# Retention and a three-way maxout layer on one core: a weight load cut in two, and two blocks' small loads moved up the SP queue

## Chip, core and metric

The kernel runs on one core of a Trainium2 chip. The metric is the time of one execution on the device, in microseconds (us); the time of a kernel is the median of its runs. Profiles are of one execution each, with the hardware profiler.

## What is computed

Eight batches of eight heads of linear attention with decay (retention) over 576 positions and 64 channels, then a feed-forward layer whose hidden unit is the largest of three projections. The weights arrive as 64-bit floats, everything else as 32-bit floats.

```python
batch, n_heads, seq, head_dim = (8, 8, 576, 64)
n_tokens, d_model, d_ff = (4608, 512, 768)
...
scores = scale * np.matmul(q, k.transpose(0, 1, 3, 2))
Dmat = np.where(rel >= 0, gamma[:, None, None] ** rel[None, :, :], 0.0)
ret = scores * Dmat[None, :, :, :]
attn = np.matmul(ret, v)
...
h = np.maximum(np.maximum(x @ w1, x @ w2), x @ w3)
return h @ w_out
```

`x` is the attention's output with the heads side by side: 4608 rows of 512.

## The kernel before

**Blocks and tiles.** The 4608 rows are cut into 36 blocks of 128 rows, and four blocks make one tile of 512 rows. `ffn(t)` is the feed-forward layer of tile t. While it runs, `steps(t + 1)` works on the attention of the next tile's four blocks, in twelve places: place n is a list of steps, emitted ahead of the n-th part of `ffn(t)`. All engines run what is emitted for them strictly in that order. Tile 0's blocks 0 to 3 are done before any feed-forward work. Blocks 4 to 7 (called a, b, c, d in `steps(1)`) are done during `ffn(0)`, and this is also the time in which the weights are loaded and converted.

**Loads.** All loads of q, k, v and of the weights are issued by SP, one after the other.

- `load` (L247) brings k, q and v of blocks 0 to 3, and k and v of later blocks, 256 KB each, in rows of 256 bytes.
- `load_blocks` (L229) brings q and k of blocks from 4 on once more, in 32x32 pieces as VectorE's transpose wants them: sixteen transfers of 32 KB a block (eight of q, eight of k), in rows of 128 bytes. Their two buffers each are used in turn, so block 7's wait for block 5's transposes and block 6's for block 4's.
- `load_weights(n)` (L520, L516) goes on by n pieces in a list. Two pieces are a pair: of w1, w2 or w3, a pair is 256 columns, 1 MB, loaded by one transfer in rows of 2 KB when its first piece comes up; the second piece then loads nothing. Of w_out, a pair is two transfers of 512 KB. There are nine pairs of w1, w2, w3 and three of w_out, and four buffers for pairs. Each conversion of a pair asks for the next two pieces (`product`).
- A transfer carries one of eight semaphores in turn, and its issue waits until the transfer eight before it has landed.

**Conversion.** `convert_all` makes 32-bit floats of a pair of 64-bit ones, in small steps spread over `ffn(0)`: on ACT two activations that read the loaded words (L695, L696) and two more (L702, L704); on VectorE L703, L708, L713 and L728. The first three pairs are converted by halves (one piece at a time), all others whole. The first pair's first half is needed by the first product of the feed-forward layer (`up_plain`, L858).

**Attention of blocks 0 to 3.** TensorE transposes k and q (`kt`, `qt`, L286), ACT copies them to SBUF (L287), TensorE makes scores (L300), VectorE masks them (L216), and TensorE makes the new state (`kv`, L368) and the output (`o`, L409, and L424 for the part that comes from the state).

**Attention of blocks from 4 on.** `transposes` is two transposes on VectorE (`kT`, `qT`, L216). `decay` scales v: of blocks 4 and 5 in one operation on VectorE (L254), of later blocks in eight operations on ACT (L204, one a head), which wait in a list that `scale` empties a few at a time, in between the conversion's activations; `scores` first empties what is left. Then, for each head in turn, TensorE makes the scores (`sk`, L322) and the state's increment (`kv`, L325), which needs that head's scaled v. Blocks 6 and 7 come one after the other, just ahead of the last product of the layer, `downs_plain` (`down`, L845), which goes through w_out's pairs in order with sixteen matmul instructions a pair; the attention's outputs of blocks 6 and 7 (`o`, L439 and L446) stand after the first pair.

**Order on SP.** At the start: k, q, v of blocks 0 and 1; k and q of block 2; the first weight pair; v of block 2; k, q, v of block 3; the next two pairs. Later, from the last pair of w3 on: w_out's first pair; k and v of block 6; w_out's second pair; k and v of block 7; the sixteen small loads of block 6; w_out's third pair; the sixteen of block 7; then block 8's.

Of the kernel before, what the change touches and what calls it, by code (L numbers as in the profile page):

```python
# [98 lines left out]
def kernel(  # L99
# [14 lines left out]
    nc = tc.nc  # L114
    P = 128
# [7 lines left out]
    CPT = NT // C  # L123
# [62 lines left out]
    def spans(g):  # L186

        row = 0
        while row < C:
            b, pos = divmod(g * C + row, S)  # L190
            n = min(C - row, S - pos)
            yield row, b, pos, n
            row += n
# [24 lines left out]
    def load_blocks(g, *blocks):  # L218
        for n, src in (("q", q), ("kx", k)):

            if 0 in blocks:
                raws[n, g] = raw.tile([P, H, D // 32, 32], FP32, tag=n, name=n + "raw", bufs=2)
            t = raws[n, g]
            for blk in blocks:
                b, pos = divmod(g * C + 32 * blk, S)
                c, e = divmod(blk, 2)
                for a in range(2):
                    r = D * c + 32 * a
                    nc.sync.dma_start(  # L229
                        t[r:r + 32, :, e, :],  # L230
                        src[b, :, pos:pos + 32, 32 * a:32 * a + 32].rearrange("h p i -> p h i"))

    def load(g, names="kqv"):
        if g >= BY_PE and "q" in names and ("q", g) not in raws:
            load_blocks(g, *range(C // 32))
        for n, src in (("k", k), ("q", q), ("v", v)) if g < BY_PE else (("k", k), ("v", v)):
            if n not in names:
                continue
            bufs = {"k": 3, "q": 2, "v": 4}[n]
            pool, bufs = (raw0, 1) if n != "v" and g < BY_PE and g % (bufs + 1) == bufs else (raw, bufs)  # L240
            if n == "v":
                t = vpool.tile([C, H, D], FP32, tag="v", name="vraw")
            else:
                t = pool.tile([C, H, D], FP32, tag=n, name=n + "raw", bufs=bufs)
            raws[n, g] = t
            for row, b, pos, m in spans(g):
                nc.sync.dma_start(t[row:row + m], src[b, :, pos:pos + m, :].rearrange("h p d -> p h d"))  # L247
# [252 lines left out]
    WS = (moe_w1, moe_w2, moe_w3)  # L500
    units = [(fp, i) for fp in range(NF // 2) for i in range(3)]
# [5 lines left out]
    def load_weights(n):  # L507
        for _ in range(n):
            if not to_load:
                return  # L510
            i, fb = piece = to_load.popleft()
            if fb % 2 == 0:
                bits[i, fb // 2] = wraw.tile([P, 2, DM], I64, tag="bits", name="bits")
            t = bits[i, fb // 2]
            if i == "out":
                nc.sync.dma_start(t[:, fb % 2, :], moe_w_out[fb * P:(fb + 1) * P, :])  # L516
                continue
            if fb % 2:
                continue
            nc.sync.dma_start(t[:].rearrange("p e f -> p (e f)").rearrange("p (n f) -> p n f", f=2 * P),  # L520
                              WS[i][:, fb * P:(fb + 2) * P].rearrange("(n p) f -> p n f", p=P))

    def seven_forms(order):

# [148 lines left out]
    def convert_all():  # L673
# [3 lines left out]
        class Two:  # L677
# [38 lines left out]
            def product(self, e):  # L716
                mant, expo = self.of(e, self.mant, self.expo.bitcast(FP32))
                if self.i == "out":
                    w = w_out[:, self.fp]
                    both_of = w.rearrange("p e f -> p (e f)")  # L720
                else:
                    w = w_up[self.i][:, 2 * self.fp:2 * self.fp + 2, :]
                    both_of = w.rearrange("p e (n f) -> p n e f", f=P)
                    if e is both:
                        mant, expo = (x.rearrange("p (n e f) -> p n e f", e=2, f=P) for x in (mant, expo))
                    else:
                        both_of = both_of[:, :, e, :]
                nc.vector.tensor_tensor(both_of, mant, expo, op=ALU.mult)  # L728
                for n in (0, 1) if e is both else (e,):
                    w_sb[self.i, 2 * self.fp + n] = w[:, n, :]  # L730
                    load_weights(1)
# [121 lines left out]
    def up_plain(t, h, fb, i, *parts):  # L853
        ps = (ps_x, ps_y)[fb % 2].tile([P, NT], FP32, tag="xy"[fb % 2], name="up")

        def products(a, b):
            for dc in range(NDC):
                nc.tensor.matmul(ps[:, a:b], lhsT=w_sb[i, fb][:, dc * P:(dc + 1) * P], rhs=xT[t][:, dc, a:b],  # L858
                                 start=dc == 0 and a == 0, stop=dc == NDC - 1, skip_group_check=len(parts) > 0)

        def maximum():
            if i > 0:
                nc.vector.tensor_tensor(h[:, fb, :], h[:, fb, :], ps[:], op=ALU.max)
            else:
                nc.scalar.copy(h[:, fb, :], ps[:])

        ends = [0, *parts, NT]
        steps = [partial(products, a, b) for a, b in zip(ends, ends[1:])]
        steps.pop(0)()
        return (*steps, maximum)  # L870
# [113 lines left out]
    load(0)  # L984
    load(1)
    load(2, "kq")
    load_weights(2)
    load(2, "v")
    load(CPT - 1, "kqv")
    load_weights(2)  # L990
    load_weights(2)
    decay(0)
# [35 lines left out]
    def steps(t):  # L1028


        todo = [[] for _ in range(3 * CPT)]

        def at(n, *what):
            for step, *args in what:
                if step is values:
                    if args[0][0] < NG:
                        todo[n].append(partial(values, *args))
                elif args[0] < NG:
                    todo[n].append(partial(soon, partial(step, *args)) if step is load else partial(step, *args))

        if t == 1:
            a, b, c, d = range(CPT, 2 * CPT)
            at(0, (load, a, "kv"))
            at(1, (load_blocks, a, 0, 1, 2, 3))
            at(2, (load_weights, 2))
            at(3, (load, b, "kv"), (load_blocks, b, 0, 1, 2, 3), (decay, a))
            at(4, (transposes, a))
            at(5, (load, c, "kv"), (decay, b), (transposes, b))
            at(6, (load, d, "kv"), (decay, c), (load_blocks, c, 0, 1, 2, 3))
            at(7, (values, [a, b]), (decay, d), (convert, 2), (load_blocks, d, 0, 1, 2, 3))  # L1050
            at(8, (transposes, c))
            at(9, (load, d + 1))
            at(10, (values, [c, d]), (load_blocks, d + 2, 0, 1))
            at(11, (decay, d + 1), (load_blocks, d + 2, 2, 3), (load, d + 2), (transposes, d + 1))
            return todo
        for n in range(0, CPT, 2):
            a, b, m = CPT * t + n, CPT * t + n + 1, 6 * (n // 2)
            first_pair = t == 2 and n == 0
            s = m + 2 if first_pair else m + 1
            at(m - (n > 0), (transposes, b))  # L1060
            if first_pair:
                at(m, (decay, b), (load, a + 2))
            at(s, (scores, a), (scores, b), (load, b + 2))
            at(s + 1, (decay, a + 2))
            at(s + 2, (decay, b + 2))
            at(s + 3, (values, [a, b]), (transposes, a + 2), (load, a + 4))
        return todo

    for t in range(N // NT):
        work = ffn(t)  # L1070
        for todo in steps(t + 1):
            for step in todo:
                step()
            next(work, None)
# [51 lines left out]
```

## Time and profile before

| | |
|---|---|
| median of 3 runs | 740.69 us (738.68 to 741.06) |
| the profiled execution's own time | 739.48 us |
| its span | 737.8 us |
| granted TensorE clock | 1.0 of full speed |
| attention of blocks 0 to 3 and the first pair's conversion | 0 to 27 us |
| `ffn(0)`, with blocks 4 to 7 and the conversion of all weights | 22 to 118 us |
| tiles 1 to 8 | 118 us to the end |

How to read it: the span is what the profile covers, from the first to the last instruction, and the execution's time is a little longer. PE is TensorE's matmuls, PEld its weight loads, DVE is VectorE, SPq the issuing of transfers on SP. A row of the timeline has start and duration in us, the engine, line and operation, what it writes and reads, the sizes, and how often it ran in a row; in brackets stands how long the engine had been idle before it, and who released it. A row of the waits has who waited for whom, the us in total, how often, and the longest. An issue on SP takes as long as SP is held up by it, waits included.

The page's share of the transfers and of VectorE and ACT in 40 slices of the span (18.4 us each, in tenths):

```profile
DVE  4899799999886895689658876787768966893676
ACT  4795905554345524544354535543555255424441
DMA  9878544414251415141424243322514151000001
```

The first six slices, up to 118 us, hold the most transfers, and VectorE and ACT are at their fullest there.

### The profile page before, as it was taken

What the parts mean: (1) busy time and instruction counts of PE and PEld (TensorE: products, weight loads), DVE (VectorE), ACT (ScalarE), POOL (GpSimd) and SP (SyncE); (2) the same over time, 40 slices, a digit from 0 to 9 for tenths busy, and PEclk for the clock granted to TensorE, in tenths of its full rate; (3) what the DMA queues carried; (4) which work ended last, traced back from release to release, by engine and by line L of the source; (5) the groups of instructions that cost most, each with busy time, mean ns of one, the idle gap of its engine ahead of it and who ended that gap; (6) DMA issues with size and microseconds to landing.
All of it is one profiled execution on the core that took longest, in us unless ns stands there. A gap on an engine that the chain in (4) does not pass through costs nothing.

```text
span 737.8 us, 17257 instructions
## 1 busy us (share of the span) xinstructions
PE 731.2 (99%) x6916; PEld 604.5 (82%) x6916; DVE 575.3 (78%) x1050; ACT 352.2 (48%) x734; POOL 37.1 (5%) x43
## 2 busy tenths in 40 slices
PE   9999999999999999999999999999999999999998
PEld 7644546888888888888888888888888888888887
DVE  4899799999886895689658876787768966893676
ACT  4795905554345524544354535543555255424441
POOL 2000010112000100010000000000100010000000
DMA  9878544414251415141424243322514151000001
GB/s 234 270 225 248 113 85 119 83 27 92 70 103 23 95 40 105 36 84 48 102 51 77 47 109 60 65 52 59 114 26 91 44 106 26 1 29 30 1 1 57
DMA packets 234832, 59.90 MB, mean 81 GB/s; under 512 B 220672, under 2 KB 228864, under 8 KB 234752
## 3 DMA queue, kind: packets, MB, share of 16 engines
q1 hardware_dynamic: 233776, 58.76, 35.3%
q8 instruction: 54, 0.88, 0.5%
q14 instruction: 26, 0.21, 0.1%
q10 hardware_dynamic: 976, 0.04, 0.1%
HBM read 49.32 MB, written 9.44 MB: 80 GB/s over the span
## 4 chain that ended last, share of the span: by engine, by line
PE 91%; SPq 5%; DMA 2%; DVE 1%; issue 0%; DVEq 0%
PE a L833 20%; PE b L833 17%; PE c L833 9%; PE di L666 7%; PE d L833 6%; PE e L833 6%; PE dhc L666 5%; PE up L858 3%; PE deg L666 3%; SPq L229 3%; PE sk L322 3%; PE down L845 3%; PE o L439 2%; PE o L446 2%; PE dfd L666 2%; PE dx L573 1%
## 5 line engine op out<-in xcount | busy, mean ns | idle before, releaser
L821 DVE TENSOR_TENSOR part<-part 128x512 f32<-128x512 f32 x168 | 117.8, 701 | 85.9 <-ACT part L818 83.3
L818 ACT COPY part<-b 128x512 f32<-128x512 f32 x120 | 70.3, 586 | 163.2 <-PE b L833 162.7
L821 DVE TENSOR_TENSOR h<-h,part 128x512 f32<-128x512 f32 x120 | 83.2, 694 | 23.8 <-ACT h L818 19.8
L204 ACT ACTIVATE vraw<-vraw,gk 128x64 f32<-128x64 f32 x240 | 77.0, 347 | 11.3 <-DMA vraw<-in_v_dram 11.3
L818 ACT COPY part<-a 128x512 f32<-128x512 f32 x96 | 56.3, 586 | 51.5 <-PE a L833 51.1
L833 PE MATMUL b<-s,n 128*128 128x256 f32 x288 | 73.9, 379 | 0.0
L858 PE MATMUL up<-xT,w 128*128 128x512 f32 (+2 forms) x160 | 62.9, 552 | 0.0
L833 PEld LDWEIGHTS b<-s,n 128*128 128x128 f32 x288 | 54.7, 190 | 7.4
L858 PEld LDWEIGHTS up<-xT,w 128*128 128x128 f32 x160 | 28.8, 190 | 31.5 <-issue 28.6
L339 POOL TENSOR_TENSOR s<-s,gs_of 64x512 f32<-64x512 f32 x24 | 26.4, 1101 | 552.3 <-DVE s L337 512.1
L833 PE MATMUL c<-xT,w 128*128 128x256 f32 x192 | 51.3, 389 | 0.0
L655 ACT COPY k<-di 128x256 f32<-128x256 f32 x49 | 18.3, 373 | 68.5 <-PE di L666 42.1
L833 PE MATMUL d<-s,w 128*128 128x256 f32 x192 | 49.8, 380 | 0.0
L833 PE MATMUL b<-xT,n 128*128 128x256 f32 x192 | 49.3, 379 | 0.0
L833 PE MATMUL a<-xT,w 128*128 128x256 f32 x192 | 49.3, 379 | 0.0
L833 PE MATMUL a<-s,w 128*128 128x256 f32 x192 | 49.3, 379 | 0.0
L833 PE MATMUL a<-xT,n 128*128 128x256 f32 x192 | 45.4, 379 | 0.0
L833 PE MATMUL e<-xT,w 128*128 128x256 f32 x192 | 45.4, 379 | 0.0
L833 PEld LDWEIGHTS e<-xT,w 128*128 128x128 f32 x192 | 36.5, 190 | 5.4 <-issue 0.5
L833 PEld LDWEIGHTS b<-xT,n 128*128 128x128 f32 x192 | 36.5, 190 | 5.0
L833 PEld LDWEIGHTS a<-xT,n 128*128 128x128 f32 x192 | 36.5, 190 | 5.0
L833 PEld LDWEIGHTS a<-xT,w 128*128 128x128 f32 x192 | 36.5, 190 | 5.0
(183 smaller groups left out, 1378.6 us busy)
## 6 DMA issues: line engine op xcount, KB each, us to landing
bits<-in_moe_w_dram SPq DMA_DIRECT2D x9, 1024.0 KB, 7.9
kraw<-in_k_dram SPq DMA_DIRECT2D x32, 256.0 KB, 3.1
vraw<-in_v_dram SPq DMA_DIRECT2D x32, 256.0 KB, 3.9
qraw<-in_q_dram SPq DMA_DIRECT2D x256, 32.0 KB, 2.1
kxraw<-in_k_dram SPq DMA_DIRECT2D x256, 32.0 KB, 2.1
out_dram<-osb SPq DMA_DIRECT2D x56, 128.0 KB, 1.7
bits<-in_moe_w_out_dram SPq DMA_DIRECT2D x6, 512.0 KB, 6.0
out_dram<-osb SPq DMA_DIRECT2D x7, 256.0 KB, 2.0
```

What stands on the lines that cost most here:

```text
L204: scaling.popleft()()
L229: nc.sync.dma_start(t[r:r + 32, :, e, :], src[b, :, pos:pos + 32, 32 * a:32 * a + 32].rearrange("h p i -> p h i"))
L322: nc.tensor.matmul(s[half(c), h, :], lhsT=kT[half(c), h, :], rhs=qT[half(c), h, :], start=True, stop=True)
L339: nc.gpsimd.tensor_tensor(new, new, factor, op=ALU.mult)
L439: nc.tensor.matmul(o[m][half(c), n, u, :], lhsT=vds[g][half(m), h, :], rhs=sts[g][half(m), h, :], start=n == 0 and u == 0, stop=place(g, m ...
L655: nc.scalar.copy(place, a)
L666: nc.tensor.matmul(banks[chain], lhsT=hidden(h, order, b, late_ones)[:, e], rhs=late["V"][v][:, e], start=begins and e == 0, stop=chain no ...
L818: nc.scalar.copy(of[step], ps[step[0]][:])
L821: nc.vector.tensor_tensor(of[dst], a, b, op=op)
L833: nc.tensor.matmul(ps[chain][:, e, :], lhsT=factor(w, 2 * fp + e), rhs=xS[t][x], start=n == 1 and e == 0, stop=ends, skip_group_check=True)
L845: nc.tensor.matmul(b[:], lhsT=h[:, fb, m * P:(m + 1) * P], rhs=w_sb["out", fb], start=fb == blocks[0], stop=fb == blocks[-1])
L858: nc.tensor.matmul(ps[:, a:b], lhsT=w_sb[i, fb][:, dc * P:(dc + 1) * P], rhs=xT[t][:, dc, a:b], start=dc == 0 and a == 0, stop=dc == NDC - ...
```

## The change

```diff
@@ load_weights
-            if fb % 2:
+            single = (fb // 2, i) == units[0]
+            if fb % 2 and not single:
                 continue
-            nc.sync.dma_start(t[:].rearrange("p e f -> p (e f)").rearrange("p (n f) -> p n f", f=2 * P),
-                              WS[i][:, fb * P:(fb + 2) * P].rearrange("(n p) f -> p n f", p=P))
+            wide = 1 if single else 2
+            nc.sync.dma_start(
+                t[:].rearrange("p e f -> p (e f)").rearrange("p (n f) -> p n f", f=2 * P)[:, :, fb % 2 * P:(fb % 2 + wide) * P],
+                WS[i][:, fb * P:(fb + wide) * P].rearrange("(n p) f -> p n f", p=P))
@@ the start
     load(2, "kq")
-    load_weights(2)
+    load_weights(1)
     load(2, "v")
-    load(CPT - 1, "kqv")
+    load(CPT - 1, "kq")
+    load_weights(1)
+    load(CPT - 1, "v")
     load_weights(2)
     load_weights(2)
@@ steps(1)
             at(4, (transposes, a))
-            at(5, (load, c, "kv"), (decay, b), (transposes, b))
-            at(6, (load, d, "kv"), (decay, c), (load_blocks, c, 0, 1, 2, 3))
-            at(7, (values, [a, b]), (decay, d), (convert, 2), (load_blocks, d, 0, 1, 2, 3))
+            at(5, (load_blocks, c, 0, 1, 2, 3), (load, c, "kv"), (decay, b), (transposes, b), (load_blocks, d, 0, 1, 2, 3))
+            at(6, (load, d, "kv"), (decay, c))
+            at(7, (values, [a, b]), (decay, d), (convert, 2))
```

**Edit 1.** The first pair of weights (of w1) is loaded in two transfers of 512 KB, each in 512 rows of 1 KB. The first keeps the pair's place, the second comes after block 3's q. The first half's conversion waits for the first transfer only, the second half's for the second.

**Edit 2.** The sixteen small loads of block 6 move ahead of block 6's k and v, and those of block 7 come right behind these. SP's order becomes: w_out's first pair; sixteen small loads of block 6; k and v of block 6; sixteen of block 7; w_out's second pair; k and v of block 7; w_out's third pair; then block 8's.

On TensorE, VectorE, ACT and GpSimd the instructions and their order are the same as before. SP has one transfer more.

## The prediction

> **What bounds the kernel now.** I read the page first, then the waits of TensorE in the first 125 us, then the timelines of TensorE, SP and ACT around the waits found.
>
> ```profile
> span 737.8 us, 17257 instructions
> PE 731.2 (99%) x6916; PEld 604.5 (82%) x6916; DVE 575.3 (78%) x1050; ACT 352.2 (48%) x734; POOL 37.1 (5%) x43
> PE sk L322 <- DVE qT L216: 1.8, 1, 1.8
> PE kt L286 <- DMA kraw<-in_k_dram: 0.4, 1, 0.4
> ```
>
> TensorE is busy for 731.2 of 737.8 us, and the waits name only two that the edits can reach. Both edits change nothing but the order of SP's transfers, so they can win at most those two.
>
> Is TensorE also dense between them? A 128x512 matmul comes every 0.432 us (the 32 of w_out's later pairs take 13.84 us, from 104.44 to 118.28). From 27.19 to 62.65 us it runs the equivalent of 82 of them, 35.4 us of work in 35.46 us. So a delay or gain anywhere in the first 118 us goes through to the end one for one.
>
> ```profile
> 17.15 0.63 PE L286 MATMUL kt<-ident,kraw 128*128 128x128 f32 x4 [0.38 <-DMA kraw<-in_k_dram]
> 17.71 0.69 PE L368 MATMUL kv<-vd,kraw 128*64 128x64 f32 x16
> 94.04 0.33 PE L322 MATMUL sk<-qT,kT 64*64 64x64 f32 x4 [1.76 <-DVE qT L216]
> 95.35 7.13 PE L845 MATMUL down<-w_out,h 128*128 128x512 f32 x16
> ```
>
> The first wait is for block 3's k, the second for block 7's transposed q and k.
>
> **Edit 1, the first weight pair in halves.** Before, 1 MB of weights goes ahead of block 3's k; after, 0.5 MB. The weights stream at 396 GB/s (windows, 19 to 26 us), so k comes about 1.3 us before its 17.02 us. The score group before `kt` starts at 15.61 and takes 1.09, so TensorE is free at 16.70: 0.45 us could be won. But what is late next? Behind `kt` and `kv` stands `o` (L409), whose second product needs the second mask of VectorE (L216, two from 16.80 to 18.09). VectorE hands to TensorE in 0.14 us (`qT` ends at 93.90, `sk` starts at 94.04), so that product starts at 18.23 at the earliest; it started at 18.34. Gain 0.1 us.
>
> What can it cost? The second half now stands behind block 3's q, whose issue ends at 14.59, and lands about where that q landed before, near 17.9, since as many bytes are ahead of it. ACT took that half at 18.30. It may be 0.6 us late before the copy of `qT` (19.89) holds up the scores. The halves have rows of 1 KB, which the trace doesn't show. By the 256-byte rows of k, q and v (272 GB/s in 4 to 8 us) a half takes 1.9 us, by the 2 KB rows (396 GB/s) 1.3; I take 1.4, nearer the long ones. Bounds of the edit: -0.45 (the mask does not decide) to +0.6 (the half lands at the slow rate behind a late q); I take -0.1.
>
> The Trainium skill speaks against the split ("DMA: Bandwidth & Descriptors", Bandwidth: batch transfers to 1 MiB or more, as smaller ones lose efficiency). The w_out halves of 512 KB, which land 1.2 to 1.4 us apart in this trace, don't show it; by the rule the edit would lie nearer its +0.6 than my -0.1.
>
> **Edit 2, the block loads of 6 and 7.** SP before:
>
> ```profile
> 59.15 0.92 SPq L516 DMA_DIRECT2D bits<-in_moe_w_out_dram  x2
> 60.11 0.67 SPq L247 DMA_DIRECT2D kraw<-in_k_dram  x1
> 60.89 1.54 SPq L247 DMA_DIRECT2D vraw<-in_v_dram  x1
> 62.97 4.03 SPq L516 DMA_DIRECT2D bits<-in_moe_w_out_dram  x2
> 67.51 1.47 SPq L247 DMA_DIRECT2D vraw<-in_v_dram  x1
> 86.75 3.90 SPq L229 DMA_DIRECT2D kxraw<-in_k_dram  x8
> ```
>
> Block 7's 16 small loads stand last; they end at 90.65, land at 92.51, and the transposes follow. The edit moves all 32 small loads up: block 6's sixteen ahead of block 6's k and v (60.11), block 7's sixteen ahead of w_out's second pair, block 7's k and v and the third pair. So block 7's q and k come early, and block 6's v, the second pair, block 7's v and the third pair come late. Walked along SP (landings are those of single transfers in the trace):
>
> - The eighth small load waits for the transfer eight before it, the first w_out pair's second half, which lands at 66.71 (the same rule shows before: a small load waits to 86.37, when the third pair lands). From there before, eight more loads ended 4.28 us later (90.65); so block 6's end at 71.0.
> - k and v of block 6: 0.5 us each, landing 2.9 us after the issue ends (100.09+0.53, landed 103.47). v lands at 75.0 instead of 69.8.
> - Sixteen loads behind a k and v took 9.1 us (100.71 to 109.83). Block 7's end at 81.3.
> - Then the second pair, block 7's k and v. A pair landed 5.25 us after the last small load's issue (81.12 to 86.37), k and v 0.9 us each after it (72.27, 73.16, 74.06). Block 7's v lands at 88.3 instead of 74.06.
>
> Who waits for that v? ACT scales it in eight pieces (L204), in a fixed order among the weight conversions:
>
> ```profile
> 72.33 0.83 ACT L204 ACTIVATE vraw<-vraw,gk 128x64 f32<-128x64 f32 x3
> 80.91 0.81 ACT L204 ACTIVATE vraw<-vraw,gk 128x64 f32<-128x64 f32 x3
> 81.63 1.13 ACT L695 ACTIVATE expo<-bits 128x1024 f32<-128x1024 bf16 x1
> 83.80 0.83 ACT L204 ACTIVATE vraw<-vraw,gk 128x64 f32<-128x64 f32 x3
> 86.76 0.81 ACT L204 ACTIVATE vraw<-vraw,gk 128x64 f32<-128x64 f32 x3
> 89.65 0.35 ACT L204 ACTIVATE vraw<-vraw,gk 128x64 f32<-128x64 f32 x1
> ```
>
> Eight pieces are block 6's, up to the second of the group at 80.91; its third, at 81.39, is block 7's first, and the one at 89.65 is its last. ACT had no idle time from 72.3 to 92.2, so from the first to the end of the last (90.00) it is 8.6 us of work that stays. After: block 6's v costs ACT 75.0-72.3=2.7 us, so it reaches block 7's first piece at 84.1, and waits there to 88.4. The last piece ends at 97.0. Head 7 of block 7's `kv` (L325) needs it and stands ahead of `down` on TensorE. So `down` starts at about 97.1 instead of 95.35: **+1.7 us**.
>
> The old wait does not even go. Queued behind ACT's first piece of block 7 is the second w_out pair's conversion: its two activations, from 81.63 to 83.92 before, end at 90.9 after. VectorE's `mant` (L708) needs the second and stands ahead of block 7's transposes: 1.15 us, then 0.6 for a maximum, then 0.65 and 0.67: `qT` at 94.0, as before.
>
> The other delays have cover. w_out's second pair is ready at about 97.0 and used from 106 on; the third was ready at 106.6 and used from 111.4; block 6's last piece is ready at 84.0, before its scores at 91.12.
>
> Bounds of the edit: below, the whole wait goes, 94.04-92.08 = 1.9, so -1.9. Above, SP stalls: single small loads took 1.4 us longer than their 0.45 (76.72 to 78.64) or 0.95 (92.67). Two more such stalls than the walk has, +2.8, would make +4.5; none, +0.5. I take +1.7, as the walk goes by rows of like neighbours.
>
> **Sum.** -0.1+1.7=+1.6 us. The profiled execution has a span of 737.8 and a time of 739.48 us: it becomes 739.4 and 741.1. The median of the runs is 740.69, 1.2 above the profiled one, so I forecast 742.3 us, slower by 0.2%. About 0.3% (2.2 us) is what a measurement of this kernel tells from no change: its three runs alone span 2.4 us.
>
> **Rivals.**
> - *The wait simply goes.* It needs block 7's v by about 83.4, so that ACT's last piece is done at 92.1. For it: ACT's order could hide a v that is only a little late. Against it: sixteen loads at 0.49 us stand between block 6's v and the second pair, so even without a stall v can't land before 87. Result -1.9-0.1: 738.7 us. It decides from a landing of block 7's v under 83.4 on.
> - *A draw.* v lands at 86.6, because the pair lands faster than behind earlier loads; ACT ends at 95.3, where TensorE was anyway. Result -0.1: 740.6.
> - *SP stalls more.* For it: of the four groups of eight small loads from 69 to 91 us, one took 5.39 instead of 3.90. Two stalls more bring v to 91 and the end of `kv` to 100: 745.1, slower by over 0.3%.
> - *The first pair's second half is late* by more than its 0.6 us of cover: up to +0.7 on the forecast, 743.0. Against it: as many bytes are ahead of it as were ahead of a transfer that landed at 17.86.
>
> **How the numbers follow.** Forecast 0.58, draw 0.13, the wait goes 0.09, more stalls 0.15, late half 0.05. The range 739.8 to 744.2 holds the forecast with its own spread of about one stall (1.0 to 1.4) and the runs' spread, the draw, the late half and the lesser stalls; it leaves out most of the won wait and the upper stalls. Over 0.3% slower: a quarter of the forecast (0.15), the stalls (0.15) and a bit of the late half and noise: 0.33. Over 0.3% faster: the won wait, -2.0, reaches it only with noise, 0.05. Within: 0.62.
>
> **What would show it.** In the changed kernel: `kt` (L286) without its 0.38 us wait but `o` (L409) no more than 0.15 us earlier; ACT idle before a piece of L204 twice, about 2.7 us near 72.3 and 4 us near 84, both released by `vraw`; `kv` of block 7 waiting for ACT; `down` starting near 97. I am wrong if block 7's v lands before 84, if `down` starts before 94, or if SP is past block 7's small loads before 78.

## The result and the profile after

The changed kernel takes 744.52 us (median of 11 runs, 741.5 to 747.88) beside 739.94 us for the kernel before (11 runs, 737.78 to 741.51): ratio 1.0066, 95% interval 1.0047 to 1.0085. That is 4.6 us slower, where 1.6 was forecast. The profiled execution took 742.75 us, 3.3 more than the one of before.

First the waits that the forecast walked to. The waits of TensorE in the changed kernel (engine, line waited for, then us in total, times, longest):

```profile
PE kv L325 <- ACT vraw L204: 1.6, 1, 1.6
PE sk L322 <- DVE qT L216: 1.6, 1, 1.6
```

The wait for block 7's transposes is still there, and one for the scaled v has come to it. The `kt` wait is gone from this profile. SP's queue in the timeline of the changed kernel (start, duration, engine, line, operation):

```profile
66.48 4.02 SPq L229 DMA_DIRECT2D kxraw<-in_k_dram  x8
...
75.87 4.98 SPq L229 DMA_DIRECT2D kxraw<-in_k_dram  x8
80.95 0.87 SPq L516 DMA_DIRECT2D bits<-in_moe_w_out_dram  x2
81.92 0.38 SPq L247 DMA_DIRECT2D kraw<-in_k_dram  x1
82.34 0.58 SPq L247 DMA_DIRECT2D vraw<-in_v_dram  x1
```

Block 7's small loads are issued by 80.85, and its v, issued at 82.34, landed at 87.94 (before: 74.06). The timeline of ACT, same kernel, with the idle time and its releaser in brackets:

```profile
74.55 0.83 ACT L204 ACTIVATE vraw<-vraw,gk 128x64 f32<-128x64 f32 x3 [2.27 <-DMA qraw<-in_q_dram]
...
87.97 0.35 ACT L204 ACTIVATE vraw<-vraw,gk 128x64 f32<-128x64 f32 x1 [4.22 <-DMA vraw<-in_v_dram]
...
96.23 0.35 ACT L204 ACTIVATE vraw<-vraw,gk 128x64 f32<-128x64 f32 x1
```

ACT waits for the v of block 6 (74.48; the view names another load that landed last), then for that of block 7, and scales the last piece at 96.23. The conversion behind block 7's first piece is late with it, and block 7's transposes stand behind that conversion on VectorE, as the forecast had it. The timeline of VectorE:

```profile
90.53 1.23 DVE L711 SCALAR_TENSOR_TENSOR mant<-frac,mant 128x1024 f32<-128x1024 int32 x1 [1.66 <-ACT mant L699]
...
92.90 0.67 DVE L216 STREAM_TRANSPOSE qT<-qraw 128x512 f32<-128x512 f32 x1
```

So both waits of TensorE come from the late v. TensorE then:

```profile
16.59 0.66 PE L286 MATMUL kt<-ident,kraw 128*128 128x128 f32 x4
...
93.72 0.33 PE L322 MATMUL sk<-qT,kT 64*64 64x64 f32 x4 [1.58 <-DVE qT L216]
...
96.64 0.48 PE L325 MATMUL kv<-vraw,kraw 64*64 64x64 f32 x4 [1.64 <-ACT vraw L204]
97.04 8.45 PE L848 MATMUL down<-w_out,h 128*128 128x512 f32 x16
...
107.45 14.00 PE L848 MATMUL down<-w_out,h 128*128 128x512 f32 x32
```

`down` starts at 97.04, 1.69 later than the 95.35 of before. The forecast's walk ended there, at 97.1. But the next `down` starts at 107.45 instead of 104.44: 3.01 later. The sixteen products between took 8.45 us, and 7.13 before. Nothing delayed them from outside. The record of the granted clock shows 3.413 us at half speed there. Here are the windows of the changed kernel, cut where that record changes and every 3.413 us before (busy us of PE, PEld, DVE, ACT, POOL with counts, then the granted clock, DMA share and GB/s):

```profile
89.49:92.91 3.42, 2.64 (x68) 1.40 (x66) 2.38 (x4) 3.39 (x6) 0.00 (x0) 1.00 0.57 116
92.91:96.32 3.41, 1.28 (x60) 1.16 (x60) 3.38 (x5) 3.41 (x7) 0.00 (x0) 1.00 0.36 56
96.32:99.73 3.41, 3.10 (x7) 1.46 (x8) 2.88 (x5) 2.45 (x4) 1.01 (x1) 0.50 0.68 139
99.73:103.15 3.42, 3.42 (x9) 1.52 (x8) 3.19 (x4) 1.07 (x4) 1.48 (x2) 1.00 0.66 117
```

From 92.91 to 96.32 TensorE worked only 1.28 us, between two short waits; the next 3.413 us run at half clock. The span grew by 3.2: 1.69 up to `down`, nearly all by the late v (the last 0.40 us of work before `down` ran at half clock already), 1.32 by the sixteen slow products, 0.2 elsewhere.

Runs of the changed kernel, sorted by their mean granted clock, point to this as most of what the forecast missed. One window at half clock lowers the mean over 741 us by 0.0023 and should cost up to 3.413/2 = 1.7 us, half of the work that TensorE does in it:

| mean granted clock | windows at half clock | runs | median time, us |
|---|---|---|---|
| 1.0 | 0 | 1 | 741.5 |
| 0.998 | 1 | 2 | 743.1 |
| 0.995 | 2 | 6 | 744.8 |
| 0.993 | 3 | 2 | 747.1 |

A run in which v lands later can have more windows and a longer direct delay as well, so the steps of this table are not the price of the windows alone; the filled kernels below take the two apart. With 1.7 us taken off for each window, the 11 runs have a median of 741.5. The runs of the kernel before that were made beside the experiments have medians of 739.5 to 740.1 among those at clock 1.0, and 0.4 to 0.7 windows a run on average, where the changed kernel has 1.8.

### The profile page after: what moved, and what is told of

Same layout as the page of the kernel before. It is cut to its first block, busy times and chain, and to the rows that moved or that the text cites. A ratio compares the mean times of both kernels' runs of the same rounds, so it can differ in the third digit from the quotient of the medians.

```text
span 741.0 us, 17260 instructions
## 1 busy us (share of the span) xinstructions
PE 732.4 (99%) x6916; PEld 604.5 (82%) x6916; DVE 575.8 (78%) x1050; ACT 352.3 (48%) x734; POOL 37.2 (5%) x43
## 4 chain that ended last, share of the span: by engine, by line
PE 92%; SPq 3%; DVE 2%; DMA 2%; ACT 1%; issue 0%; DVEq 0%
PE a L836 20%; PE b L836 17%; PE c L836 9%; PE di L669 7%; PE d L836 6%; PE e L836 6%; PE dhc L669 5%; PE up L861 3%; PE deg L669 3%; PE down L848 3%; PE sk L322 3%; SPq L229 3%; PE o L439 2%; PE o L446 2%; PE dfd L669 2%; PE dx L576 1%
## 5 line engine op out<-in xcount | busy, mean ns | idle before, releaser
L836 PEld LDWEIGHTS a<-s,w 128*128 128x128 f32 x192 | 36.5, 190 | 5.0
```

What stands on the lines that cost most here:

```text
L836: nc.tensor.matmul(ps[chain][:, e, :], lhsT=factor(w, 2 * fp + e), rhs=xS[t][x], start=n == 1 and e == 0, stop=ends, skip_group_check=True)
```

## Experiments

Each ratio is against the kernel before, measured in turns with it on the same chip. Theory at the outset: the late v costs 1.7 us directly, and the two short waits bring windows at half clock for the rest. Rivals: the first edit costs something; SP's stalls or an early stage carry the loss.

**Each edit alone.** e1_first_edit has the first weight pair in halves and the old order of the small loads; e2_second_edit the reverse. Not shown are e1's lines in `load_weights`, which are the same as in the change.

```diff
 e1_first_edit, against before
-    load_weights(2)
+    load_weights(1)
     load(2, "v")
-    load(CPT - 1, "kqv")
+    load(CPT - 1, "kq")
+    load_weights(1)
+    load(CPT - 1, "v")
 e2_second_edit, against before
-            at(5, (load, c, "kv"), (decay, b), (transposes, b))
-            at(6, (load, d, "kv"), (decay, c), (load_blocks, c, 0, 1, 2, 3))
-            at(7, (values, [a, b]), (decay, d), (convert, 2), (load_blocks, d, 0, 1, 2, 3))
+            at(5, (load_blocks, c, 0, 1, 2, 3), (load, c, "kv"), (decay, b), (transposes, b), (load_blocks, d, 0, 1, 2, 3))
+            at(6, (load, d, "kv"), (decay, c))
+            at(7, (values, [a, b]), (decay, d), (convert, 2))
```

> The first edit alone (the first weight pair in halves; the small loads in their old order). Theory: the loss is the second edit's, through block 7's late v, and the clock drop that follows the wait. Then this kernel has the same 1.9 us wait before block 7's scores as the kernel before, granted clock 1.0, and is 0.1 us faster: 739.8 against 739.9, ratio 0.9995 to 1.0005. Rival: the second half of the first pair, landing at 18.5 behind block 3's q, costs part of the loss; then 1 to 2 us slower and lower clock values in its runs.

> The second edit alone. Theory: it carries the whole loss: the last product of the first layer starts about 1.7 us late (near 97), its start runs at half clock in most runs, ratio 1.005 to 1.008. Rival (the loss is shared with the first edit, or comes from the two together): ratio under 1.004.

Measured: e1_first_edit 740.51 us (12 runs), ratio 0.9994 (0.997 to 1.0017), `down` at 95.37. e2_second_edit 745.37 us (6 runs), ratio 1.0061 (1.0041 to 1.0082); in its profile `down` starts at 98.66, the waits for block 7's transposes and for v are 2.3 and 1.6 us, and all six runs have a mean clock of 0.995, two windows each. The second edit carries the whole loss.

**Keeping TensorE busy in the two waits.** Block 6's last score products are repeated behind its scores, and block 7's ahead of its last head's `kv`, 100 products at each place in e3_filled, 24 in e7_filled12. No value that is kept changes.

```diff
 e7_filled12, against after (e3_filled: range(50))
+            if g == 2 * CPT - 2 and h == H - 1 or g == 2 * CPT - 1 and h == H - 2:
+                for _ in range(12):
+                    for c in range(2):
+                        nc.tensor.matmul(s[half(c), h, :], lhsT=kT[half(c), h, :], rhs=qT[half(c), h, :],
+                                         start=True, stop=True)
```

> The changed kernel with TensorE kept at work in its two waits: 100 repeats of head 7's score products of block 6 after that block's scores, and 100 repeats of head 6's of block 7 ahead of that block's head 7, 1.5 us each, hidden in waits of 1.58 and 1.64 us. They add no result: each overwrites the same place with the same values. Theory: the loss beyond 1.7 us is the granted clock, which falls to one half for 3.4 us because TensorE was idle; then the clock is 1.0 in nearly all runs, and the time is that of the changed kernel's one run at clock 1.0, near 741.5, ratio 1.002 to 1.003. Rival: the clock falls for another reason (heat, the chip); then clocks of 0.993 to 0.998 stay and the ratio is 1.006 as for the changed kernel.

> As e3_filled, with 24 repeats in the place of 100 at both points, since the repeats took 0.03 us each, not 0.015 (the 100 took 5.9 us): 1.4 us in each wait. Theory: clock 1.0, down near 97.1, 741 to 742 us on a chip where the kernel before takes 739.9; ratio 1.002 to 1.003, and a narrow spread. Rival (the clock is not set by TensorE's idling): ratio 1.006.

Measured: e3_filled 751.31 us (5 runs, 750.56 to 751.95), ratio 1.0142 (1.0118 to 1.0167). That is a miss: each product is two rows of the trace (7316 rows of PE instead of 6916), and a row by itself takes 0.03 us, about twice what one takes among the others. So 100 products took 5.9 us instead of 1.5, the filling overran the waits, and `down` started at 106.64, 9.6 later than in the changed kernel. But the clock was 1.0 in all five runs, and 751.31 - 9.6 = 741.7. Against the 95.35 of the kernel before, `down` is 11.3 late, and 751.31 - 11.3 = 740.0, which is what the kernel before takes on that chip in its runs at clock 1.0 (740.05). At full clock the delay of `down` is the whole loss.

e7_filled12, with a quarter of the filling, took 742.74 us (12 runs), ratio 1.0034 (1.0012 to 1.0057), at clock 1.0 in 10 of 12 runs, where the changed kernel had 1 of 11. About half of the loss goes when TensorE has something to do, although nothing starts earlier (the intervals of the two ratios, 1.0012 to 1.0057 and 1.0047 to 1.0085, overlap a little).

The runs at clock 1.0 have a median of 742.5, 1 us over the 741.5 of above. The profile of e7_filled12, a run of 744.96 us at clock 1.0, doesn't lay this on the filling: it fits in both waits with time to spare. It shows a later v. The timelines of ACT and TensorE in e7_filled12:

```profile
91.50 0.35 ACT L204 ACTIVATE vraw<-vraw,gk 128x64 f32<-128x64 f32 x1 [4.32 <-DMA vraw<-in_v_dram]
...
97.27 0.33 PE L322 MATMUL sk<-qT,kT 64*64 64x64 f32 x4 [2.81 <-DVE qT L216]
...
100.49 7.13 PE L853 MATMUL down<-w_out,h 128*128 128x512 f32 x16
```

Block 7's v comes 3.5 us later than in the profile of the changed kernel, and `down` starts 5.1 later than before, at full clock. How much of the 1 us the other runs owe to this was not measured.

**Taking the late v away.** Three kernels move loads or the scaling. The first has k and v of block 6 ahead of its small loads, and w_out's second pair and block 7's k and v ahead of block 7's.

```diff
 e4_v_first, against after
-            at(5, (load_blocks, c, 0, 1, 2, 3), (load, c, "kv"), (decay, b), (transposes, b), (load_blocks, d, 0, 1, 2, 3))
-            at(6, (load, d, "kv"), (decay, c))
+            at(5, (load, c, "kv"), (decay, b), (transposes, b), (load_blocks, c, 0, 1, 2, 3))
+            at(6, (load, d, "kv"), (decay, c), (load_blocks, d, 0, 1, 2, 3))
 e5_scale4, against after: four pieces of v at a time instead of three
-                    scale(3)
+                    scale(4)
 e6_v_first_scale4: e4_v_first and e5_scale4 together
 e8_both_v, against after: both blocks' k and v side by side
-            at(5, (load_blocks, c, 0, 1, 2, 3), (load, c, "kv"), (decay, b), (transposes, b), (load_blocks, d, 0, 1, 2, 3))
-            at(6, (load, d, "kv"), (decay, c))
+            at(5, (load_blocks, c, 0, 1, 2, 3), (load, c, "kv"), (load, d, "kv"), (decay, b), (transposes, b), (load_blocks, d, 0, 1, 2, 3))
+            at(6, (decay, c))
```

> The first edit, and the small loads in a third order: k and v of block 6 ahead of its sixteen small loads, then w_out's second pair, k and v of block 7, the sixteen of block 7, w_out's third pair. Theory: what counts is that each v is there when ACT comes to it and that block 7's q and k are there by 89. Block 7's v then lands near 81, its small loads near 87, the third pair near 90.5, so ACT's last piece of v ends near 93.5 instead of 90.0, and down starts near 93.7 instead of 95.35: 1.5 to 1.8 us faster than before, ratio 0.998. Rival: any move of the small loads ahead of a w_out pair costs what it wins: ratio 1.000 or more.

> The changed kernel with ACT taking four pieces of v at a time instead of three, so block 7's eight pieces all stand ahead of the third w_out pair's conversion (four of them behind the second pair's). Theory: the wait of kv for ACT's last piece (1.6 us) is the time that the last piece spends behind two conversions; with four at a time the last piece ends near 92, so that wait is gone. The scores still wait for block 7's transposes, behind the second pair's conversion, to about 94.4. down starts near 95.8 instead of 97.0: ratio 1.001 to 1.003, and fewer half-clock windows. Rival: the late v itself is the loss, wherever its pieces stand; then nothing changes, 1.006.

> The third order of the small loads (block 6's behind its own k and v, block 7's behind its own k and v and ahead of w_out's third pair) and four pieces of v at a time. Theory: in that order the third pair came too late and ACT's last piece of v stood behind it (4.0 us of waiting by kv). With four at a time it doesn't; block 7's q and k land near 91, its scores start near 92.2, down near 93.5 instead of 95.35, no half-clock window: 1.5 to 2 us faster than the kernel before, ratio 0.997 to 0.999. Rival: TensorE finds another wait in the place of this one (the third pair's conversion, now some 5 us later, holds up down): ratio 1.000 or more.

> The changed kernel with k and v of block 7 right behind those of block 6, ahead of block 7's small loads. Theory: ACT's 4.2 us wait for block 7's v goes, but w_out's second pair is then still late (landing near 88 to 89) and ACT waits for that instead, with the same pieces of v behind it: down between 96 and 97.5, ratio 1.003 to 1.006. Rival (the late v alone is the loss): ACT's last piece near 92.7, down near 94 to 95, ratio under 1.001.

Measured: e4_v_first 744.29 us (8 runs), ratio 1.004 (1.0011 to 1.007), a miss. The v is early now, but the third w_out pair, behind block 7's small loads, is late, and the last piece of v stands behind its conversion. The timeline of ACT in e4_v_first:

```profile
98.43 1.13 ACT L698 ACTIVATE expo<-bits 128x1024 f32<-128x1024 bf16 x1 [5.43 <-DMA bits<-in_moe_w_out_dram]
...
100.56 0.33 ACT L204 ACTIVATE vraw<-vraw,gk 128x64 f32<-128x64 f32 x1
```

ACT idles 5.43 us for the pair, and the last piece of a v that landed long before is scaled at 100.56; `kv` waits 4.0 us. In that profile everything was some 3 us late from the start as well, by a wait of 1.8 us for block 3's k and one of 1.8 us for ACT's copy of block 3's `qT`. The second is the first edit's: ACT stood waiting for the first weight pair's second half until 22.17, with that copy behind it. The timeline of TensorE in e4_v_first:

```profile
24.00 1.16 PE L300 MATMUL s<-qT,kT 64*128 64x128 f32 x16 [1.80 <-ACT qT L287]
```

With scale(4) the eighth piece goes with the second group, ahead of that conversion. e6_v_first_scale4, the same order with it, took 739.4 us (12 runs), ratio 0.9976 (0.9957 to 0.9996). In its profile TensorE waits neither for block 7's transposes nor for v, and `down` starts at 94.11. So place in ACT's queue and landing both decide; either alone isn't enough. e5_scale4, with the late v kept, took 742.79 us (12 runs), ratio 1.0031 (1.0011 to 1.005): `kv` doesn't wait, but block 7's transposes are later, so the one wait is 2.9 us, and in its profile `down` starts at 96.89, hardly better than 97.04. Two things add up there: three more pieces of v ahead of the second pair's conversion (0.7 us), and a v that landed at 89.1, 1.2 later than in the profile of the changed kernel. Better too is the clock: 1.1 windows a run instead of 1.8. e8_both_v took 745.32 us (10 runs), ratio 1.0051 (1.0025 to 1.0076), as expected: the w_out pair takes the place of the late v (ACT waits 4.2 us for it), and its profile has three windows at half clock.

**What e6's gain is made of.** e10_order_scale4 has e6's order and scale(4) without the first edit, e11_before_scale4 only scale(4) on the kernel before, e9_before_filled the 24 repeats in the first place on the kernel before, and e12_best_again is e6 again, on another chip.

```diff
 e9_before_filled, against before
+            if g == 2 * CPT - 2 and h == H - 1:
+                for _ in range(12):
...
 e11_before_scale4, against before
-                    scale(3)
+                    scale(4)
 e10_order_scale4: e11_before_scale4, and against before
-            at(5, (load, c, "kv"), (decay, b), (transposes, b))
-            at(6, (load, d, "kv"), (decay, c), (load_blocks, c, 0, 1, 2, 3))
-            at(7, (values, [a, b]), (decay, d), (convert, 2), (load_blocks, d, 0, 1, 2, 3))
+            at(5, (load, c, "kv"), (decay, b), (transposes, b), (load_blocks, c, 0, 1, 2, 3))
+            at(6, (load, d, "kv"), (decay, c), (load_blocks, d, 0, 1, 2, 3))
+            at(7, (values, [a, b]), (decay, d), (convert, 2))
```

> The kernel before with 24 of block 6's last score products repeated behind its scores, in the place where TensorE waits 1.76 us for block 7's transposes; a repeat took 1.51 us for 46 rows in the 24-repeat run of the changed kernel, so it fits in the wait and delays nothing (the extra products change no value that is kept). Theory (a fixed grid of 3.413 us windows, and a window in which TensorE worked less than some 1.3 to 1.55 us is followed by one at half clock): the kernel before, too, lost 0.6 windows a run on average in the other jobs, 1.0 us, all of it from this one wait when the grid and the length of the wait fall badly; filled, the granted clock is 1.0 in nearly all runs and the mean falls by about 1 us: ratio 0.9975 to 0.9995, few runs over 742. Rival (the kernel before loses its windows elsewhere, near the start of the run, or for reasons that have nothing to do with idle time): the runs at 0.998 and 0.995 stay as frequent, ratio 0.9995 to 1.001.

> The kernel before with the order k and v of block 6, its sixteen small loads, w_out's second pair, k and v of block 7, its sixteen small loads, third pair, and with scale(4), without the first edit: the run that beat both kernels less the halved weight pair. Theory (the first edit is worth nothing, the gain is the wait at block 7's scores and the half-clock windows that it can bring): ratio 0.996 to 0.999, granted clock 1.0, no wait of TensorE for block 7's scores. Rival (part of that gain was the first edit): 0.9995 to 1.001.

> The kernel before with scale(4) alone. Theory: in the kernel before the wait at block 7's scores ends with its small loads (landed 92.51 us), which this leaves where they are, so the wait stays at about 1.8 us, kv has no wait to lose, and the time is the same: ratio 0.999 to 1.0015. Rival (the earlier scaling of v is what made the run with the other order fast): 0.996 to 0.999.

> The version with both edits' ideas that beat both kernels (halved first pair; order k and v of block 6, its small loads, second pair, k and v of block 7, its small loads, third pair; scale(4)), once more. Theory: the order removes the wait at block 7's scores (1.8 us) and, with it, its half-clock windows; the halved pair makes block 3's k a little earlier, and so the windows after a late k at about 19 us rarer, which without it came in 5 of 12 runs: ratio 0.996 to 0.9985, mean granted clock below 0.9985 in at most 2 of 12 runs. Rival (the halved pair does nothing, and the fewer windows of its first measurement were luck): ratio 0.998 to 1.0, windows in 4 to 6 of 12 runs.

Measured: e9_before_filled 740.35 us (12 runs), ratio 1.0007 (0.9989 to 1.0025), with 4 of 12 runs still at 0.998: the rival holds, the windows of the kernel before don't come from the wait at block 7's scores. e11_before_scale4 740.29 us (12 runs), ratio 1.0003 (0.9987 to 1.0018): scale(4) alone does nothing. e10_order_scale4 739.69 us (12 runs), ratio 0.9986 (0.997 to 1.0002). That run was expected at clock 1.0, and 5 of 12 weren't (0.998 or 0.995). Its profile is one of these and shows a place where the kernel before, the same up to there, can lose its windows too; no profile of the kernel before itself fell on such a run. The timeline of TensorE in e10_order_scale4, then its windows, cut as above:

```profile
20.14 1.08 PE L286 MATMUL kt<-ident,kraw 128*128 128x128 f32 x4 [3.58 <-DMA kraw<-in_k_dram]
```

```profile
15.52:18.93 3.41, 1.04 (x16) 0.85 (x16) 0.59 (x2) 0.59 (x2) 0.00 (x0) 1.00 0.25 59
18.93:22.34 3.41, 2.20 (x24) 1.90 (x26) 3.38 (x7) 3.14 (x7) 1.61 (x2) 0.50 0.90 206
22.34:25.76 3.42, 3.42 (x28) 2.76 (x26) 0.32 (x1) 1.42 (x4) 0.00 (x0) 0.50 0.98 314
```

Block 3's k landed at 20.01, and `kt` waited 3.58 us instead of the 0.38 in the profile of before; two windows at half clock follow. This is the wait that the first edit is aimed at. e12_best_again, with that edit, took 738.29 us (12 runs, 737.77 to 739.09), ratio 0.997 (0.9956 to 0.9984). Over both measurements of this version none of 24 runs has a clock of 0.998 or less; without the first edit 5 of 12 have, on a third chip. The version with both ideas beats both kernels; it takes 0.3% less than the kernel before.

## Why the prediction was right and wrong

- **Edit 1, -0.1: right for the profile it was made from, too small for the runs.** `kt` runs at 16.59 without a wait, and the products of `o` begin 0.54 earlier but end only 0.15 earlier (19.05 instead of 19.20), as the forecast had it. The second half landed at 18.49, not 17.9, without a cost in this profile. By the rule of the Trainium skill ("DMA: Bandwidth & Descriptors", Bandwidth: transfers of 1 MiB or more) the halves should lose; the later landing may be that, but the time of e1_first_edit, 0.9994, does not show it. What the forecast overlooked: 0.38 us was one draw. The five profiles without the edit have this wait at 0.4 to 3.6 us, those with it at 0 to 1.8, most at 0; the value of the edit lies in the long draws, and was seen only once the other wait was gone.
- **Edit 2, the walk along SP and ACT: right, each step within 0.5 us.** In the profile, block 6's small loads end at 70.5 (71.0 forecast), its v lands at 74.48 (75.0), block 7's small loads end at 80.85 (81.3), its v lands at 87.94 (88.3). ACT idles 2.27 and 4.22 us (2.7 and 4), the last piece ends at 96.6 (97.0), the scores of block 7 start at 93.72 (94.0), and `down` at 97.04 (97.1).
- **Edit 2, the direct price of +1.7: right for the profile, where it measured 1.69 at `down`.** That profile is an early draw, though, with some luck in the match. The four other profiles with this order of loads (e3_filled, e5_scale4, e2_second_edit, e7_filled12) have block 7's v at 88.8, 89.1, 89.6 and 91.5 instead of 87.94, and in the two where nothing but v sets it, `down` starts at 98.66 and 100.49. Runs with the clock taken out, 741.5 against 739.5 to 740.1, say 1.4 to 2.0.
- **The sum: here it failed.** It took "a delay goes through to the end one for one" from a TensorE that is dense at full clock and priced nothing that waiting does to the pace after it. Two waits, in the profile 1.6 us each with 1.3 us of small products between, brought one to three windows at half clock in ten of eleven runs. The term left out is (1.8 - 0.4 to 0.7 windows) x 1.7 = 1.9 to 2.4 us. 1.4 to 2.0 and 1.9 to 2.4 make 3.3 to 4.4; 4.6 was measured, and the rest is not placed.
- **The range** went up to 744.2 for SP's stalls alone; with a term for the clock, 0 to 3 windows (5.1 us), the measured time would have been inside.
- **The rivals.** That the wait simply goes, and the draw: neither, v landed after 83.4 and after 86.6. That SP stalls more is not what happened in the profile of the changed kernel, where SP was 0.4 us faster than the walk; but the profile of e7_filled12, with v at 91.5, `down` at 100.49 and 744.96 us at full clock, is this rival nearly to the number (91, 100, 745.1). So it is a part of the spread of the runs, and how large a part was not measured. The late second half doesn't show in the profile of the changed kernel either, but in seven of the nine profiles with the first edit TensorE waits for ACT's copy of block 3's `qT`, which stands behind that half's conversion: 0.2 to 0.8 us, and 1.8 in e4_v_first. In none of the five without the edit does it. The clock was no rival at all.

What stays open: why the profiled pattern meets so many runs. Laid on the rows of its profile at every phase, a grid of 3.413 us gives the changed kernel a window with less than 1.42 us of work (midway between the 1.28 and 1.55 of the section on the clock below) in 4 of 10 phases, e2_second_edit in nearly all and the kernel before in none (1.65 at least). For e2_second_edit (6 of 6) that fits; for the changed kernel (10 of 11) the runs must mostly have longer waits than the profile has. The four other profiles with this order, with v 0.9 to 3.5 us later, agree with that; it wasn't tried apart.

## What to carry to other kernels

On a TensorE that is busy throughout, as here, a wait has two prices: its length, and the half-clock windows it can bring, up to 1.7 us each. So add up TensorE's work over any 3.4 us around a wait, and compare the granted clock of the runs before explaining a difference of medians. A load moved ahead in a queue pushes back what it overtakes: follow the latest of these to the engine whose fixed order it blocks (here ACT, where moving one small piece ahead of a conversion decided between 1.004 and 0.9976). And a walk that fits one profile to half a microsecond has fitted one draw: the same load landed over a range of 3.5 us in five profiles.

## What the hardware showed unexpectedly

**The clock follows a fixed grid, and the work in a window decides.** The stretches of the clock record are whole multiples of 3.413 us: 92.16 = 27 windows, 641.71 = 188. The Trainium skill ("TensorE: Matmul & The Clock Gate", Part 1: The HAM clock gate) gives a free-running window of 3413 ns and half rate after an idle one; the length and the halves agree with the traces. On the same page of the Trainium skill, the section "HAM oscillation" asks for no idle gaps over about 3.4 us. Here the longest gap in the changed kernel's profile was 1.64 us, and the clock fell; the measurement decides. From full clock it fell after windows with 0.62, 1.04, 1.16, 1.27 and 1.28 us of TensorE work (e4_v_first, e10_order_scale4, e2_second_edit, e8_both_v, after), and held after 1.60 to 1.78 (e1_first_edit, e4_v_first, e5_scale4, e7_filled12, e9_before_filled, e11_before_scale4). One of those that held, in the windows of e5_scale4, with a single gap of 2.9 us split by the grid:

```profile
90.99:94.40 3.41, 1.65 (x66) 1.02 (x64) 2.01 (x3) 3.38 (x8) 0.00 (x0) 1.00 0.53 95
94.40:97.82 3.42, 2.24 (x66) 1.75 (x67) 3.38 (x5) 3.42 (x4) 0.00 (x0) 1.00 0.36 54
```

So in these traces a window needs somewhere between 1.28 and 1.60 us of work; at half clock it stayed low after 1.38 to 2.51 us (e8_both_v, with e2_second_edit, e4_v_first and e10_order_scale4 between) and rose after 3.10 and 3.42 (the changed kernel, e2_second_edit), which is the same bound if work at half clock counts half (1.26 and 1.55). That it counts so is a reading of the numbers and was not tried by itself.

**Early loads vary more than one profile shows.** In kernels that are the same up to there, the wait for block 3's k was 0.4 us in one profile and 3.6 in another; in e10_order_scale4 that k took 2.87 us to issue, and 0.95 in the profile of before.
